# Rolling DVE's and ACT's code of a cached-attention decode kernel into loops, as PE's is

## The chip, the cores and the metric

The kernel runs on one core of a Trainium2 chip. The metric is device time in microseconds for one execution, the median of three runs. A core has five engines that run their own instruction streams and meet through semaphores: PE (TensorE, matrix multiplies), DVE (VectorE), ACT (ScalarE), POOL (GpSimd) and SP (SyncE, which here only issues DMAs). Sixteen DMA engines move data between HBM and the on-chip memory SBUF; a large transfer is split over all sixteen.

## The reference

The reference computes two independent one-token attention blocks, A and B, and concatenates their outputs:

```python
B, Sq, D = 8, 1, 1024;  H, Sk, Dh = 32, 4096, 128
q = (x @ wq).reshape(B, Sq, H, Dh).transpose(0, 2, 1, 3)
scores = einsum("bhqd,bhkd->bhqk", q, k_cache) * Dh ** -0.5
p = softmax(scores, axis=-1)
o = einsum("bhqk,bhkd->bhqd", p, v_cache)
out = o.transpose(0, 2, 1, 3).reshape(B, Sq, H * Dh) @ wo
```

Everything is bf16. The two K caches and the two V caches hold 8 x 32 x 4096 x 128 elements each, 268 MB. Each of them is read once.

## The kernel before

**Slots.** A slot is one batch element b and one group of four heads (`HP = 4`). Eight slots, one for each b, make a group; eight groups (`NG = 8`) make one of the two blocks; so there are 2 x 8 x 8 = 128 slots. For a slot, the K rows of its four heads are one load of 4 MB into one of two buffers `kbuf` (`load_k`, L271), its V rows one load of 4 MB into one of two buffers `vbuf` (`load_v`, L278). Each head takes 32 partitions, and each partition holds 128 of its 4096 positions, 32 KB in one piece.

**What a slot does.** DVE multiplies K by the query in two halves (`multiply`, L315-321, 64 positions of 128 elements for each partition at a time) into `prod`. PE adds up the products by 16 matmuls with an identity (`add_up`, L323) into PSUM, and DVE reduces the last eight columns for each position (`reduce`, L338) into `score`. The softmax is spread over DVE (maximum, L347-352) and ACT (exponentials with their sums, L356). PE multiplies the probabilities with V (`pv`, L370, 32 matmuls), ACT copies the result out of PSUM (L386), PE gathers each head's part (`gather`, L388), and DVE scales it by the inverse sum (`heads`, L399; `invert`, L366) into `on`. Once in a group, `project` (L406) multiplies `on` by the group's four heads of `wo` into the PSUM tile `acc`, and DVE adds that to the running sum `osum` (L418); for a block's last group the sum goes into `orow`, and two small DMAs write it out. Once in a group, too, ACT copies the next group's queries from `qT` into `qg` (`pick_q`, L294), and every four slots PE and ACT spread four queries over the partitions (`make_qbc`, L299).

**The order.** It is written out by hand in one Python loop over n (L435-501). Work of slots n, n-1, n-2 and n-3 is interleaved. Within a pass DVE's order is: first half of the multiply for n, reduce and softmax for n-1, the projection's sum (in passes with n % 8 == 2 and n > 8), second half of the multiply for n, reduce, `heads` of n-2, `invert` of n-1. The K load of slot n+2 needs the buffer of slot n, so it is issued by SP when the second half of the multiply is done; the V load needs the buffer that `pv` has read. All large loads go through SP's queue, in the order of the program. The second block's `wq` takes two turns of the K buffers just before slot 35 (`n == L1`, L443-450): the second of these two loads needs the buffer that slot 34's second multiply reads.

**Semaphores.** `Program.add` records each operation with what it depends on; `Program.finish` (L62) gives each engine's signalled operations consecutive counts and reduces each operation's dependences to waits for counts.

**Loops.** The instruction streams of all engines but PE are straight-line code for all 128 slots. PE alone has loops: slots 3 to 34 (`L0` to `L1`) and 35 to 122 (`L1` to `L2`) repeat every eight slots, so PE runs the first stretch as 4 passes and the second as 11 passes over a body of eight slots (`rolled`, L523). A wait in a body is for a count that rises from pass to pass, held in a register to which a fixed amount is added before the wait. `Program.rolled` (L104) derives these amounts from the recorded waits.

## Time and profile before

| | |
|---|---|
| median of 3 runs | 2588.9 us (2588.84 to 2588.95) |
| profiled execution | 2588.76 us |
| its span, from the first to the last instruction | 2586.4 us |
| mean granted TensorE clock | 0.79 of full speed |
| read from HBM | 1107.33 MB, 428 GB/s over the span |
| DVE first multiply operations (L319) | 256, mean 4.42 us, idle before them 951.9 us in total, for K loads |
| DVE waits ahead of the running sum (L418) | 85.0 us in 14 groups, for PE's projection |
| loads of K: issue to landing, median | 28.5 us |
| loads of V: issue to landing, median | 32.4 us |

The page's busy times are those of an engine's own instructions; register, branch and semaphore instructions and the issue of DMAs are not counted as busy. A share of the DMA engines is the mean over sixteen. The kinds of DMA traffic are told apart by queue: loads and stores that the program issues, and "instruction", by which the engines' own code arrives. All times are on the profiled execution's clock, from the span's start.

### The profile page before, as it was taken

Reading aid. Unit: us, or ns where it says so; the run is one execution under the profiler, and the core shown is the slowest. Engines: PE = TensorE matmul, PEld = TensorE weight load, DVE = VectorE, ACT = ScalarE, POOL = GpSimd, SP = SyncE. Lnnn points to the kernel's source line nnn. Section 1 sums busy time; section 2 is a strip of 40 time slices with the busy share of each in tenths; the row PEclk is TensorE's granted clock in tenths of the full one; section 3 lists DMA queues with packets and bytes.
Section 4 is the critical chain, followed back from the end, with each engine's and each line's share of the span. In section 5 each row is a group of like instructions: output and inputs, shape, how many; then the busy total and the mean of one; then the engine's idle time right before and its main releaser. Section 6 shows DMA issues by size and latency. Waiting matters only on the chain.

```text
span 2586.4 us, 21069 instructions
## 1 busy us (share of the span) xinstructions
PE 1594.8 (62%) x10640; PEld 303.9 (12%) x6800; DVE 1428.3 (55%) x1307; ACT 393.2 (15%) x1201; POOL 1.6 (0%) x11
## 2 busy tenths in 40 slices
PE   4666566556655656666556655665655666655666
PEld 1011111111111111111111111110111101111111
DVE  3655556565545655655556555565655565555555
ACT  0111111111111111111111111111111111111111
POOL 0000000000000000000000000000000000000000
PEclk9778778787877778778877787887877778777788
DMA  9999999999999999999999999999999999999998
GB/s 419 429 431 429 430 431 430 434 432 430 429 412 435 430 430 433 430 431 432 430 431 430 432 431 430 433 430 430 432 430 433 430 431 429 431 432 429 433 432 358
DMA packets 46454, 1107.82 MB, mean 428 GB/s; under 512 B 4512, under 2 KB 4544, under 8 KB 12752
## 3 DMA queue, kind: packets, MB, share of 16 engines
q1 hardware_dynamic: 46336, 1107.32, 99.8%
q8 instruction: 16, 0.26, 0.0%
q14 instruction: 22, 0.18, 0.0%
q10 hardware_dynamic: 80, 0.06, 0.0%
HBM read 1107.33 MB, written 0.03 MB: 428 GB/s over the span
## 4 chain that ended last, share of the span: by engine, by line
DMA 69%; DVE 25%; PE 5%; issue 0%; ACT 0%; SPq 0%
DMA kbuf<-in_A_k_cache_dram 34%; DMA kbuf<-in_B_k_cache_dram 34%; DVE prod L319 22%; PE red L329 4%; DVE score L342 1%; PE acc L413 1%; DMA vbuf<-in_B_v_cache_dram 1%; DVE rmax L347 1%; PE sps L395 1%; DVE tmax L348 0%; DVE nmax L350 0%; DVE osum L418 0%; DVE bias L352 0%; PE oacc L380 0%; PE qps L263 0%
## 5 line engine op out<-in xcount | busy, mean ns | idle before, releaser
L329 PE MATMUL red<-prod,ident 128*128 128x512 bf16 x4096 | 1201.7, 460 | 959.3 <-DVE prod L319 959.1
L319 DVE TENSOR_TENSOR prod<-kbuf,qbc 128x8192 bf16<-128x8192 bf16 x256 | 1131.3, 4420 | 951.9 <-DMA kbuf<-in_A_k_cache_dram 479.6
L356 ACT ACTIVATE prob<-score,bias 32x128 bf16<-32x128 f32 x512 | 295.1, 576 | 1015.6 <-DVE bias L352 1004.6
L386 ACT ACTIVATE osb<-oacc 128x512 f32<-128x512 f32 x128 | 76.4, 597 | 1144.7 <-PE oacc L380 1144.7
L380 PE MATMUL oacc<-vbuf,prob 128*16 128x512 bf16 x4096 | 245.5, 381 | 0.2 <-DMA vbuf<-in_B_v_cache_dram 0.2
L395 PEld LDWEIGHTS sps<-sel,osb 128*128 128x128 f32 x1024 | 135.1, 193 | 632.1 <-issue 431.9
L342 DVE TENSOR_REDUCE score<-red 128x64 f32<-128x512 f32 x256 | 175.3, 685 | 21.5 <-PE red L329 20.6
L380 PEld LDWEIGHTS oacc<-vbuf,prob 128*16 128x16 bf16 x4096 | 90.8, 89 | 565.1 <-issue 473.0
L329 PEld LDWEIGHTS red<-prod,ident 128*128 128x128 bf16 x256 | 33.1, 129 | 1024.9 <-DVE prod L319 1020.1
L356 ACT ACTIVATION_READ_ACCUMULATOR prob<-score,bias 32x1 f32 x512 | 128.0, 250 | 0.0
L395 PE MATMUL sps<-sel,osb 128*128 128x4 f32 x1024 | 122.8, 243 | 1.6 <-ACT osb L386 1.6
L418 DVE TENSOR_TENSOR osum<-acc,osum 40x512 f32<-40x512 f32 x14 | 9.6, 682 | 85.0 <-PE acc L413 85.0
L363 PE MATMUL sps<-rsum,ones 128*128 128x4 f32 x256 | 47.2, 255 | 5.0 <-ACT prob L356 5.0
L363 PEld LDWEIGHTS sps<-rsum,ones 128*128 128x128 f32 x256 | 39.0, 192 | 22.1 <-issue 14.3
L403 DVE TENSOR_TENSOR on<-sps,rl 128x4 bf16<-128x4 f32 x128 | 21.8, 170 | 32.0 <-PE sps L363 17.8
L347 DVE TENSOR_REDUCE rmax<-score 128x1 f32<-128x128 f32 x128 | 36.7, 286 | 4.4
L348 DVE STREAM_TRANSPOSE tmax<-rmax 128x32 f32<-128x32 f32 x128 | 27.1, 212 | 4.4
L350 DVE TENSOR_REDUCE nmax<-tmax 128x1 f32<-128x32 f32 x128 | 23.8, 186 | 4.4
L352 DVE TENSOR_SCALAR bias<-nmax 128x1 f32<-128x1 f32 x128 | 19.7, 154 | 4.4
L368 DVE RECIPROCAL rl<-sps 128x4 f32<-128x4 f32 x128 | 22.0, 172 | 0.0
L269 DVE CAST qT<-qps 128x256 bf16<-128x256 f32 x2 | 0.8, 424 | 35.7 <-PE qps L263 35.7
L312 ACT ACTIVATE qbc<-bps 128x512 bf16<-128x512 f32 x32 | 18.9, 592 | 0.7 <-PE bps L307 0.7
(28 smaller groups left out, 86.3 us busy)
## 6 DMA issues: line engine op xcount, KB each, us to landing
kbuf<-in_A_k_cache_dram SPq DMA_DIRECT2D x64, 4096.0 KB, 28.5
vbuf<-in_A_v_cache_dram SPq DMA_DIRECT2D x64, 4096.0 KB, 32.4
kbuf<-in_B_k_cache_dram SPq DMA_DIRECT2D x64, 4096.0 KB, 28.5
vbuf<-in_B_v_cache_dram SPq DMA_DIRECT2D x63, 4096.0 KB, 32.4
vbuf<-in_A_wq_dram SPq DMA_DIRECT2D x2, 4096.0 KB, 17.5
wob<-in_A_wo_dram SPq DMA_DIRECT2D x8, 1024.0 KB, 30.8
kbuf<-in_B_wq_dram SPq DMA_DIRECT2D x2, 4096.0 KB, 20.2
wob<-in_B_wo_dram SPq DMA_DIRECT2D x8, 1024.0 KB, 30.8
```

The source lines that it names most:

```text
L319: P.add("dve", lambda e: e.tensor_tensor(pv, kv, qbc[:, qi, n % QT, :].unsqueeze(1).to_broadcast([128, CT, Dh]), ALU.mult), reads=[f"k{ki} ...
L329: first = e.matmul(rv, ident[:], pj[:, :, 0, :], start=True, stop=False).ins
L342: P.add("dve", lambda e: e.tensor_reduce(dst, rv, AX.X, ALU.add), writes=[f"score{n % 2}c{ch}"], banks=[f"red{i}"])
L347: P.add("dve", lambda e: e.tensor_reduce(rmax[:, i:i + 1], score[:, i, :], AX.X, ALU.max), reads=sc, writes=[f"rmax{i}"])
L348: P.add("dve", lambda e: e.transpose(tmax[:, i, :], rmax[:, i:i + 1].to_broadcast([128, SEG])), reads=[f"rmax{i}"], writes=[f"tmax{i}"])
L350: P.add("dve", lambda e: e.tensor_reduce(nmax[:, i:i + 1], tmax[:, i, :], AX.X, ALU.max), reads=[f"tmax{i}"], writes=[f"nmax{i}"])
L356: P.add("act", lambda e, pr=pr, hh=hh: e.activation(prob[pr, i, :, hh], score[pr, i, :], ACTF.Exp, bias=bias[pr, i:i + 1], scale=scale, ac ...
L363: P.add("pe", lambda e: e.matmul(sps[:, i * HP:(i + 1) * HP], ones[:], rsum[:, i, :], start=True, stop=True), reads=[f"rsum{i}h{h}" for h ...
L380: last = e.matmul(oacc[i][32 * q:32 * q + TB * HP, :], prob[:, i, j * TB:(j + 1) * TB, :].rearrange("p t h -> p (t h)"), vbuf[:, vi, j * 5 ...
L386: P.add("act", lambda e: e.activation(osb[:, i, :], oacc[i][:], ACTF.Copy), writes=[f"osb{i}"], banks=[f"oacc{i}"])
L395: last = e.matmul(sps[:, o:o + HP], osb[:, i, t * Dh:(t + 1) * Dh], sel[:, t, :], start=(t == 0), stop=(t == TB - 1))
L413: last = e.matmul(acc[32 * half:32 * half + B, :], on[:, hh, :], wob[:, hh, half * 512:(half + 1) * 512], start=(hh == 0), stop=(hh == HP ...
```

## The change

Four things change.

- The loops are kept for each engine in place of PE alone: DVE and ACT, too, run slots 3 to 34 and 35 to 122 as passes over a body of eight slots. `Program.rolled` takes the engine, and now allows for waits whose first pass differs. SP and POOL stay straight.
- What differs from group to group leaves DVE and ACT for GpSimd: the copy of the next queries (`pick_q`), and the running sum of the projections. DVE copies `acc` out of PSUM into a new tile `asb`, and GpSimd copies or adds that to `osum`, now one tile for both blocks. Only the very last projection is still added by DVE.
- `project` moves in the order from ahead of the row-sum matmul and the second multiply to behind the second multiply and its reduce.
- The output of the first block is written from SP's queue in the pass of n = 70; before, it was from ACT's, right behind the block's last projection.

The diff, cut to its core:

```diff
-        self.loops = []
+        self.loops = {e: [] for e in ENGINES}
...
-        pe = self.order["pe"]
-        for a, b, k in self.loops:
...
+        for e in ENGINES:
+            ops = self.order[e]
+            for a, b, k in self.loops[e]:
+                size = (b - a) // k
...
+                for p in range(a, a + size):
+                    if any(ops[p + i * size].sig for i in range(k)):
+                        for i in range(k):
+                            ops[p + i * size].sig = True
...
-    def rolled(self, a, b, k):
-        pe = self.order["pe"]
+    def rolled(self, eng, a, b, k):
+        pe = self.order[eng]
...
+        order = {}
         for p in range(size):
+            for key, v in sorted(value[p].items()):
+                seq = order.setdefault(key, [])
+                if not seq or v > seq[-1][1]:
+                    seq.append((p, v))
+        base, waits = {}, [[] for _ in range(size)]
+        for key, seq in order.items():
+            while seq[0][1] + step[key] <= seq[-1][1]:
+                ahead[key] = max(seq.pop(0)[1], ahead.get(key, 0))
+            was = seq[-1][1] - step[key]
+            base[key] = was
+            for p, v in seq:
+                waits[p].append((key, v - was))
+                was = v
         return ahead, base, waits
...
-        osum = sb("osum", [40, NC, 512], FP32)
+        osum = sb("osum", [40, 512], FP32)
+        asb = sb("asb", [40, 512], FP32)
...
-        P.add("dve", lambda e: e.memset(osum[:], 0.0), writes=["osum0", "osum1"])
...
         def pick_q(gi):
-            P.add("act", lambda e: e.activation(qg[:].rearrange("p h b -> p (h b)"), qT[:, c, g * HP * B:(g + 1) * HP * B], ACTF.Copy),
+            P.add("pool", lambda e: e.tensor_copy(qg[:].rearrange("p h b -> p (h b)"), qT[:, c, g * HP * B:(g + 1) * HP * B]),
...
-            dst, name = (osum, f"osum{c}") if g < NG - 1 else (orow, f"orow{c}")
-            P.add("dve", lambda e: e.tensor_tensor(dst[:, c, :], acc[0:40, :], osum[:, c, :], ALU.add),
-                  reads=[f"osum{c}"], writes=[name], banks=["acc"])
-            if g == NG - 1:
-                for half in range(2):
-                    dma("sp" if c == NC - 1 and half == 0 else "act", out[:, 0, c * D + half * 512:c * D + (half + 1) * 512],
-                        orow[32 * half:32 * half + B, c, :], [f"out{c}{half}"], "out", reads=[name])
+            end = gi == NC * NG - 1
+            dst, name = (osum, "osum") if g < NG - 1 else (orow[:, c, :], f"orow{c}")
+            if end:
+                P.add("dve", lambda e: e.tensor_tensor(dst[:], acc[0:40, :], osum[:], ALU.add), reads=["osum"], writes=[name], banks=["acc"])
+                return
+            P.add("dve", lambda e: e.tensor_copy(asb[:], acc[0:40, :]), writes=["asb"], banks=["acc"])
+            if g == 0:
+                P.add("pool", lambda e: e.tensor_copy(osum[:], asb[:]), reads=["asb"], writes=["osum"])
+            else:
+                P.add("pool", lambda e: e.tensor_tensor(dst[:], asb[:], osum[:], ALU.add), reads=["asb", "osum"], writes=[name])
+
+        def store(c):
+            for half in range(2):
+                dma("sp" if c < NC - 1 or half == 0 else "act", out[:, 0, c * D + half * 512:c * D + (half + 1) * 512],
+                    orow[32 * half:32 * half + B, c, :], [f"out{c}{half}"], "out", reads=[f"orow{c}"])
...
+        def marks():
+            return {e: len(P.order[e]) for e in ("pe", "act", "dve")}
...
             if n == L1 or n == L2:
-                P.loops.append((start, here, (n - L0) // B if n == L1 else (n - L1) // B))
+                for e, at in marks().items():
+                    P.loops[e].append((start[e], at, (n - (L0 if n == L1 else L1)) // B))
...
-                if n - 3 >= 0 and (n - 3) % B == B - 1:
-                    project((n - 3) // B)
             if 0 <= m < NS:
                 rowsum(m)
             if n < NS:
                 multiply(n, 1)
                 reduce(n, 0)
+                if n - 3 >= 0 and (n - 3) % B == B - 1:
+                    project((n - 3) // B)
...
+            if n % (NG * B) == 6 and n > B:
+                store(n // (NG * B) - 1)
+        store(NC - 1)
...
         def run(name, eng):
             ops, at = P.order[name], 0
-            if name == "pe":
-                for a, b, k in P.loops:
-                    straight(name, eng, ops[at:a])
-                    rolled(eng, a, b, k)
-                    at = b
+            for a, b, k in P.loops[name]:
+                straight(name, eng, ops[at:a])
+                rolled(name, eng, a, b, k)
+                at = b
             straight(name, eng, ops[at:])
```

More of the change, by code (lines that the diff above doesn't have):

```diff
@@ L66, in finish @@
                 d.sig = True
-        pe = self.order["pe"]
-        for a, b, k in self.loops:
-            size = (b - a) // k
-            assert size * k == b - a
-            for p in range(a, a + size):
-                if any(pe[p + i * size].sig for i in range(k)):
-                    for i in range(k):
-                        pe[p + i * size].sig = True
+        for e in ENGINES:
+            ops = self.order[e]
+            for a, b, k in self.loops[e]:
+                size = (b - a) // k
+                assert size * k == b - a, (e, a, b, k)
+                for p in range(a, a + size):
+                    if any(ops[p + i * size].sig for i in range(k)):
+                        for i in range(k):
+                            ops[p + i * size].sig = True
         counts = {}
@@ L102, in finish @@
         return counts
-    def rolled(self, a, b, k):
-        pe = self.order["pe"]
+    def rolled(self, eng, a, b, k):
+        pe = self.order[eng]
         size = (b - a) // k
         keys = [sorted(pe[a + size + p].deps) for p in range(size)]
-        step, ahead = {}, {}
+        value, step, ahead = [{} for _ in range(size)], {}, {}
         for p in range(size):
@@ L116, in rolled @@
                 assert pe[a + p].deps.get(key, vals[0] - d) == vals[0] - d, (p, key)
+                value[p][key] = vals[0] - d
             assert all(sorted(pe[a + i * size + p].deps) == keys[p] for i in range(1, k)), p
@@ L119, in rolled @@
             for key, v in pe[a + p].deps.items():
-                if key not in keys[p]:
-                    assert key not in step, (p, key, v)
-                    ahead[key] = max(v, ahead.get(key, 0))
-        last, first, waits = {}, {}, []
-        for p in range(size):
-            w = []
-            for key in keys[p]:
-                v = pe[a + size + p].deps[key] - step[key]
-                if key not in last:
-                    first[key] = last[key] = v
-                    w.append([key, None])
-                elif v > last[key]:
-                    w.append([key, v - last[key]])
-                    last[key] = v
-            waits.append(w)
-        base = {}
-        for w in waits:
-            for x in w:
-                if x[1] is None:
-                    x[1] = first[x[0]] + step[x[0]] - last[x[0]]
-                    base[x[0]] = first[x[0]] - x[1]
-                assert x[1] > 0 and base[x[0]] >= 0
+                if key not in value[p]:
+                    if key in step:
+                        value[p][key] = v
+                    else:
+                        ahead[key] = max(v, ahead.get(key, 0))
+        order = {}
+        for p in range(size):
+            for key, v in sorted(value[p].items()):
[8 more added lines that the diff above has]
+            base[key] = was
+            assert was >= 0
+            for p, v in seq:
+                waits[p].append((key, v - was))
+                was = v
         return ahead, base, waits
@@ L416, in project @@
             P.add("pe", emit, reads=[f"onb{b}" for b in range(B)] + ["wo"], banks=["acc"])
-            dst, name = (osum, f"osum{c}") if g < NG - 1 else (orow, f"orow{c}")
-            P.add("dve", lambda e: e.tensor_tensor(dst[:, c, :], acc[0:40, :], osum[:, c, :], ALU.add),
-                  reads=[f"osum{c}"], writes=[name], banks=["acc"])
-            if g == NG - 1:
-                for half in range(2):
-                    dma("sp" if c == NC - 1 and half == 0 else "act", out[:, 0, c * D + half * 512:c * D + (half + 1) * 512],
-                        orow[32 * half:32 * half + B, c, :], [f"out{c}{half}"], "out", reads=[name])
+            end = gi == NC * NG - 1
[6 more added lines that the diff above has]
+                P.add("pool", lambda e: e.tensor_copy(osum[:], asb[:]), reads=["asb"], writes=["osum"])
+            else:
+                P.add("pool", lambda e: e.tensor_tensor(dst[:], asb[:], osum[:], ALU.add), reads=["asb", "osum"], writes=[name])
[3 more added lines that the diff above has]
+                    orow[32 * half:32 * half + B, c, :], [f"out{c}{half}"], "out", reads=[f"orow{c}"])
         NS = NC * NG * B
@@ L434, in _build @@
         make_qbc(0)
+        def marks():
+            return {e: len(P.order[e]) for e in ("pe", "act", "dve")}
         for n in range(NS + 1):
             m = n - 1
-            here = len(P.order["pe"])
             if n == L0:
-                start = here
+                start = marks()
             if n == L1 or n == L2:
-                P.loops.append((start, here, (n - L0) // B if n == L1 else (n - L1) // B))
+                for e, at in marks().items():
+                    P.loops[e].append((start[e], at, (n - (L0 if n == L1 else L1)) // B))
             second = []
@@ L449, in _build @@
                     q_part(c, s, name, w)
-                start = len(P.order["pe"])
+                start = marks()
             if n < NS:
@@ L521, in straight, with rolled @@
                 one(name, eng, op)
-        def rolled(eng, a, b, k):
-            ahead, base, waits = P.rolled(a, b, k)
+        def rolled(name, eng, a, b, k):
+            ahead, base, waits = P.rolled(name, a, b, k)
             for key, val in ahead.items():
@@ L531, in rolled @@
             with eng.Fori(0, k):
-                for op, ws in zip(P.order["pe"][a:], waits):
+                for op, ws in zip(P.order[name][a:], waits):
                     for key, inc in ws:
@@ L535, in rolled @@
                         eng.wait_ge(sems[key], regs[key])
-                    one("pe", eng, op)
+                    one(name, eng, op)
         def run(name, eng):
             ops, at = P.order[name], 0
-            if name == "pe":
-                for a, b, k in P.loops:
-                    straight(name, eng, ops[at:a])
-                    rolled(eng, a, b, k)
-                    at = b
+            for a, b, k in P.loops[name]:
+                straight(name, eng, ops[at:a])
+                rolled(name, eng, a, b, k)
+                at = b
             straight(name, eng, ops[at:])
```

## The prediction

> **What bounds the kernel now.** I read the page's slices and queues first. In each fence below the first words name the row.

> ```profile
> PE 1594.8 (62%) x10640; PEld 303.9 (12%) x6800; DVE 1428.3 (55%) x1307; ACT 393.2 (15%) x1201; POOL 1.6 (0%) x11
> DMA  9999999999999999999999999999999999999998
> DMA packets 46454, 1107.82 MB, mean 428 GB/s; under 512 B 4512, under 2 KB 4544, under 8 KB 12752
> q1 hardware_dynamic: 46336, 1107.32, 99.8%
> q8 instruction: 16, 0.26, 0.0%
> q14 instruction: 22, 0.18, 0.0%
> ```

> No engine is above 62%, while the loads (q1) fill 16 DMA engines for 99.8% of the span. Then the chain of work that ended last, by engine:

> ```profile
> DMA 69%; DVE 25%; PE 5%; issue 0%; ACT 0%; SPq 0%
> ```

> Its DVE part is only how a K load gets issued: K of slot n+2 is issued 10.4 us after K of slot n has landed (16.4 to 17.8 us in the slots with a projection), and at 10.4 us there are still 18.8 us of earlier loads queued. So DVE, ACT and PE time inside a slot costs nothing. What can move the time is (a) something that occupies a DMA engine, and (b) places where a DMA engine has nothing queued.

> For (a), the two "instruction" rows. The trace's packet records give each fetch a time. The 16 KB ones (q8) are PE's. Of the 22 8 KB ones in q14, ten come every 124 to 132 DVE instructions, nine every 122 to 132 ACT instructions, three every 127 to 129 SP instructions: 8,192 B is 128 instructions. Right after each fetch exactly one load packet is long: normal 32 KB packets take 1.215 to 1.228 us; after a DVE fetch (0.325 us) it is 1.875 us, so that DMA engine loses 0.325 + 0.66 = **1.0 us**; after an ACT or SP fetch 0.31 + 0.38 = 0.7 us; after a PE fetch 1.0 + 0.5, 1.5 to 1.8 in the landings.

> Every load lands in 16 parts, one for each DMA engine. How far the last part is behind the first (my listing of landing events, us):

> ```
> load landed at   last behind first   second-last
>   396.8               2.21              1.80
>   616.0               3.10              1.73
>   725.9               0.41              0.40
>  1142.0               2.38              2.08
>  1438.9               3.39              2.32
>  1665.0               4.42              2.35
>  1961.8               5.42              3.04
>  2187.9               6.42              3.72
>  2465.4               7.42              4.39
>  2577.6 (last wo)     5.02              2.25
> ```

> The last engine steps by 1.0 at DVE's fetches (355, 605, 1125, 1380, 1625, 1877, 2135, 2378 us): all of DVE's code comes through one DMA engine. ACT's comes through another (4.39). A load is complete when its last part is, so the kernel runs at the pace of DVE's DMA engine.

> For (b): the lag collapses at 713 us and shrinks at the end, because the 15 faster engines ran dry there. The gap at 713 comes from slot 34, which holds a projection (time, length, then what DVE waited for):

> ```profile
> 702.65 0.15 DVE L352 TENSOR_SCALAR bias<-nmax 128x1 f32<-128x1 f32 x1
> 709.26 0.68 DVE L418 TENSOR_TENSOR osum<-acc,osum 40x512 f32<-40x512 f32 x1 [6.46 <-PE acc L413]
> 709.87 4.41 DVE L319 TENSOR_TENSOR prod<-kbuf,qbc 128x8192 bf16<-128x8192 bf16 x1
> ```

> ```profile
> 713.00:715.30 2.30, 0.96 (x3) 0.10 (x1) 2.04 (x4) 0.00 (x0) 0.00 (x0) 0.57 0.45 142
> ```

> DVE waits 6.46 us for the projection's matmuls before the second multiply. That multiply frees the buffer of the second wq load, issued at 714.3, while the fast engines finished the first at 713.1 (slowest 716.2). The second fence is the busy time of the stretch 713.0 to 715.3; it ends with PE's clock, the DMA share (0.45) and the rate (142 GB/s).

> **The balance before.** Against a DMA engine that has no fetch and never starves, the end comes late by: starved at 713: 3.1 us (landings 12.8 apart instead of 9.7); starved at 2543: 0.5; starved at 2567, where the last V load waits for K of slot 127 on the slowest engine: 1.9; final lag 5.0. Sum **10.5 us**. Check: 10 DVE fetches x 1.0, plus 0.4.

> **The change, part by part.**

> *DVE and ACT loop.* DVE's 32 + 88 slots become 4 + 11 passes over one body each. A body has 8 x 10 + 1 = 81 operations; the trace shows 8 waits per DVE slot (one K load, three PE, four on itself), so about 68 register adds with those of qbc and the projection, and a branch with its add: about 151 instructions. With 35 ahead, 10 between and 65 behind, DVE's code is about 412 instructions instead of 1,312: 900 fewer, 7 fetches fewer, 3 left. ACT: bodies of 74 operations and 28 for waits and branch; 293 instead of 1,210, 2 fetches left of 9. SP keeps 3, PE its own. If a body stays resident, the lags at the end are then: DVE's engine 0.3 (its lag beside the fetches) + 3 x 1.0 = 3.3; ACT's 0.5 + 2 x 0.7 = 1.9; SP's 0.5 + 2.1 = 2.6; PE's, which go round eight engines (the lengths of the long packets repeat after eight), two fetches each, 3.3 to 3.6. Slowest: 3.4.

> Does a body stay resident? DVE has no loop in this trace; the nearest row is PE's. Its body is 1,067 instructions, over four blocks of 256. Its first pass in the second loop (755 to 911 us) made four q8 fetches; from 915 to 2010, seven passes:

> ```profile
> q1 hardware_dynamic: 19629, 471.74, 100.4%
> q14 instruction: 9, 0.07, 0.0%
> q10 hardware_dynamic: 32, 0.02, 0.0%
> ```

> No q8 row at all: PE loops out of its buffer. (One packet more at 2015, one in eleven passes.) A DVE body of 1.2 of its blocks is smaller by any measure, but its buffer may be smaller too. Bounds: 0 fetches a pass (PE's row), or all of the up to 3 blocks that a body touches, 45 fetches. I take 0, since PE is the only row of a loop. [...]

> *Loop edges.* PE's taken branch lasts 0.208 us, its adds 0.032 each. On DVE and ACT between 0 and, were a fetch waited for, a few us. Cover: DVE idles 8 to 11 us for K in most slots; were that gone, 14 us more are in the queue. Cost 0.

> *Projection behind the second multiply.* In 16 slots K's issue comes back from +17 to +10.4. The cover was there but at slot 34: the second wq goes out at 707.2 instead of 714.3, 5.9 us before the fast engines run out, so the 3.1 us go. Late next is K of slot 35, which waits for PE's q matmuls (726.0), with 9.6 us to spare. The copy of acc behind the reduce costs DVE some 0.68 (the L418 row) ahead of L403 and L368; what waits for those is PE's next slot. Free.

> *GpSimd.* 16 copies of qg, 15 small adds or copies of 40x512. No such POOL row; nearest 0.30 (L217, 128x128). Between 0.1 and, held up for a whole DVE multiply, 5 us each. Slack: qg is used two slots later, osum eight; for the first qg, 29.6 (qbc done) to 33.67 (K lands), 4.1 us, and the queue behind that. Free.

> *Output of the first half from SP* in slot 70: two issues of 0.33 to 0.45 us on SP ahead of K of slot 71, whose wait is longer. Free.

> *The tail* is straight code as before. With a lag of 3.4, V's last load is issued at K127's last landing + 12.6, some 2 us before the fast engines run out: no starving.

> **Sum.** 10.5 - 3.4 = 7.1 us. The profiled execution took 2588.76 (span 2586.42), the median is 2588.9: about **2581.9**. With DVE lags of 2 to 5: 2580.5 to 2584.

> **Rivals.**

> 1. *Slower: bodies are refetched at each taken branch.* Deciding point: 7 refetches more than I count, half a block a pass. One block in 15 passes: DVE's engine lags 0.3 + 18, end 18.3 against 10.5: 2596.7. Two: 33.3, 2611.7. Three: 2627. For it: DVE's buffer is nowhere shown; a body over 151 instructions straddles two or three blocks. Against: PE's loop. 16%.

> 2. *No difference:* the engines share one ceiling, and a pause of one is filled by the others. Then only bytes count: 14 x 8 KB at 431 GB/s, 0.3 us. Against: the lag never shrinks while others idle (5.15 to 5.18 over the last four V parts). Or part of the gain is lost: more code than I count, a body refetched now and then. 2584 to 2592; 12%.

> 3. *The change doesn't do what it says* (the slot-34 gap stays since another wait is behind it): then the engines meet at 713 again, after a gap of the lag there, 2.2 (DVE's engine, two fetches), and the end lag is that of the second half, 2.3. 4.5 against 10.5: 2582.9. Inside the forecast's range.

> **How the numbers follow.** A measurement can tell 0.2%, 5.2 us, from no change. Forecast (with rival 3) 72%, own range 2579.5 to 2584: nearly all of it faster by over 0.2%. Rival 2: same, 12%. Rival 1: slower, 16%. Faster 0.71, same 0.13, slower 0.16. To hold 8 in 10 the range takes in the forecast and rival 2: 2579.5 to 2592; rival 1's prices are left out.

> **What would show it.** Right: q14 down from 22 to about 8; last part at most 4 us behind the first in the last loads; no dip at 713; DVE's wait ahead of L418 gone. Wrong: q14 at 30 or more with long packets every 156 us, or q14 down and the time unchanged (rival 2).

## The result, and the profile after

| | before | after |
|---|---|---|
| median | 2588.9 us (13 runs, 2587.85 to 2592.45) | 2582.25 us (13 runs, 2581.15 to 2585.92) |
| ratio, 95% interval | | 0.9976 [0.9969, 0.9984] |
| profiled execution | 2588.76 us | 2581.38 us |
| its span | 2586.4 us | 2579.6 us |

A second set of eight runs of the changed kernel (e12) gave a median of 2581.68 us, ratio 0.9971 [0.9961, 0.9982]. The executions of the changed kernel fall into two groups, around 2581.5 and around 2585.5 us (nine and four of the thirteen). The kernel before has such a pair too: 66 of its 83 executions on record lie between 2587.8 and 2590.5 us, 17 between 2591.5 and 2594.8. More on that under the runs of the tail.

First the page of the changed kernel: engines, the DMA engines by slice of the span, and the DMA queues.

```profile
PE 1578.8 (61%) x10640; PEld 302.2 (12%) x6800; DVE 1428.6 (55%) x1306; ACT 389.7 (15%) x1185; POOL 21.8 (1%) x42
DMA  9999999999999999999999999999999999999999
DMA packets 46440, 1107.71 MB, mean 429 GB/s; under 512 B 4512, under 2 KB 4544, under 8 KB 12752
q1 hardware_dynamic: 46368, 1107.34, 100.0%
q8 instruction: 16, 0.26, 0.0%
q10 hardware_dynamic: 48, 0.04, 0.0%
q14 instruction: 8, 0.07, 0.0%
```

The engines do the same work in the same time. What differs is q14: 8 fetches of 8 KB in place of 22 (the 32 packets that q1 has more are the first block's output, which q10 has less). By the packet records three are DVE's (105.7, 731.9 and 869.2 us), two ACT's, three SP's. A saving of 14 fetches looks like nothing in this row (0.11 MB of 1107, a share of 0.0%), and it brings nearly all of the result: without the other part of the change (e4, below) the loads still end 5.9 of the 7.3 us earlier.

What the fetches cost is seen in how far the last of a load's sixteen parts lands behind the first. The same reading as in the prediction's listing, of both kernels (us):

```
first part landed   before   after
      396.8          2.21     1.77
      616.0          3.10     1.69
      713.1          3.10     1.68
     1142 / 1139     2.38     3.25
     1439 / 1436     3.39     3.19
     1665 / 1662     4.42     3.16
     1962 / 1959     5.42     3.10
     2465 / 2462     7.42     3.09
     last wo         5.02     3.21
```

The stairs of 1.0 us are gone. The other change is at slot 34, DVE from the end of the softmax on (time, length, operation, then what it waited for), and the stretch at 713 us, whose row ends with PE's clock, the DMA share and GB/s:

```profile
701.24 0.15 DVE L353 TENSOR_SCALAR bias<-nmax 128x1 f32<-128x1 f32 x1
701.31 4.42 DVE L320 TENSOR_TENSOR prod<-kbuf,qbc 128x8192 bf16<-128x8192 bf16 x1
706.29 0.69 DVE L343 TENSOR_REDUCE score<-red 128x64 f32<-128x512 f32 x1 [0.56 <-PE red L330]
708.26 0.68 DVE L423 COPY asb<-acc 40x512 f32<-40x512 f32 x1 [1.28 <-PE acc L414]
```

```profile
713.00:715.30 2.30, 1.07 (x30) 0.56 (x23) 0.00 (x0) 0.60 (x1) 0.00 (x0) 1.00 0.99 427
```

The second multiply starts right behind the softmax, the second `wq` load goes out at 705.8 in place of 714.3, and at 713 the DMA engines move 427 GB/s where they moved 142. The loops' edges cost next to nothing; this is the line of the loop itself, the durations in ns as minimum, median and maximum:

```profile
L547 DVEq COMPARE_BRANCH  x15: 50/56/72, 233.9 to 2467.5; - x15
L547 PEldq COMPARE_BRANCH  x15: 76/208/233, 237.6 to 2471.2; - x15
L547 ACTq COMPARE_BRANCH  x15: 40/45/50, 239.3 to 2472.9; - x15
```

Fifteen branches each, and DVE's and ACT's are shorter than PE's.

### The profile page after: what moved, and what is told of

Same layout as the page of the kernel before. It is cut to its first block, busy times and chain, and to the rows that moved or that the text cites. A ratio compares the mean times of both kernels' runs of the same rounds, so it can differ in the third digit from the quotient of the medians.

```text
span 2579.6 us, 22407 instructions
## 1 busy us (share of the span) xinstructions
PE 1578.8 (61%) x10640; PEld 302.2 (12%) x6800; DVE 1428.6 (55%) x1306; ACT 389.7 (15%) x1185; POOL 21.8 (1%) x42
## 2 busy tenths in 40 slices
DMA packets 46440, 1107.71 MB, mean 429 GB/s; under 512 B 4512, under 2 KB 4544, under 8 KB 12752
## 4 chain that ended last, share of the span: by engine, by line
DMA 73%; DVE 16%; issue 10%; PE 1%; ACT 0%; DVEq 0%; SPq 0%
DMA kbuf<-in_B_k_cache_dram 36%; DMA kbuf<-in_A_k_cache_dram 35%; DVE prod L320 12%; DVE score L343 2%; DMA kbuf<-in_B_wq_dram 1%; DVE rmax L348 1%; DMA vbuf<-in_B_v_cache_dram 1%; DVE tmax L349 1%; DVE nmax L351 0%; PE red L330 0%; DVE bias L353 0%; PE qps L264 0%; PE oacc L381 0%; DVEq L550 0%; ACT prob L357 0%
## 5 line engine op out<-in xcount | busy, mean ns | idle before, releaser
L330 PE MATMUL red<-prod,ident 128*128 128x512 bf16 x4096 | 1188.1, 456 | 963.3 <-DVE prod L320 963.3
L427 POOL TENSOR_TENSOR osum<-asb,osum 40x512 f32<-40x512 f32 x12 | 15.1, 1258 | 1902.8 <-DVE on L404 1902.8
```

Of the source, the lines that this page charges most:

```text
L330: first = e.matmul(rv, ident[:], pj[:, :, 0, :], start=True, stop=False).ins
```

## The experiments

Twelve kernels ran. Times are medians of device time; where a profile decides, the time of the profiled execution is given. Ratios are to the kernel before, run beside each.

### Which part brings the time: four kernels between the two

**e1: ACT's code straight, the rest as changed.** The loops stay planned; only their emission is skipped:

```diff
-            for a, b, k in P.loops[name]:
+            for a, b, k in P.loops[name] if name != "act" else ():
```

> The changed kernel with ACT's code straight again (DVE still in loops). Theory T (each engine's code comes through one DMA engine, and the slowest DMA engine sets the time): nine ACT fetches of 0.7 us and 0.5 beside them put ACT's DMA engine 6.8 us behind at the end, against 3.3 in the changed kernel: profiled execution 2581.4 + 3.5 = 2584.9 us, last part of the late loads about 6.8 us behind the first. Rival B (only bytes count): seven fetches more are 0.06 MB at 431 GB/s, 0.15 us: 2581.5. Rival G (the whole gain is the projection's wait at slot 34, the loops bring nothing): 2581.4.

Measured: 2584.95 us, ratio to the kernel before 0.9985 [0.9976, 0.9994], profiled execution 2584.30. Last part behind the first: 2.3 at 713 us, 3.7 at 1436, 4.5 at 1662, 5.2 at 1959, 5.9 at 2185, 6.6 at 2462: steps of 0.7. For the profiled execution theory T said 2584.9, with a last part 6.8 behind; B and G are 2.8 and 2.9 us too low.

**e2: DVE's code straight, the rest as changed** (`name != "dve"`).

> The changed kernel with DVE's code straight again (ACT still in loops). T: ten DVE fetches of 1.0 us and 0.3 beside them: 10.3 us of lag at the end with nothing to level it at slot 34, so 2581.4 + 7.0 = 2588.4 us, as the kernel before, though the gap at 713 us is gone. B: 2581.5. G: 2581.4.

Measured: 2588.84 us, ratio 0.9998 [0.9989, 1.0007]: no difference from the kernel before. The lag climbs to 4.8 at 1139, 6.8 at 1662 and 9.8 at 2462.

**e3: both straight** (`if name == "pe"`): only the moves of work and of the projection are left.

> The changed kernel with both DVE's and ACT's code straight again: only the moves (queries and sums to GpSimd, projection behind the second multiply, output on SP) are left. T: DVE's DMA engine is the slowest as in the run before, ACT's 6.8 does not count: 2588.4 us, lag 10.3. B: 2581.6. G: 2581.4.

Measured: 2589.03 us, ratio 0.9999 [0.9990, 1.0008]. Its queues, and the stretch at 713 us:

```profile
q14 instruction: 22, 0.18, 0.0%
```

```profile
713.00:715.30 2.30, 2.03 (x33) 0.71 (x32) 0.00 (x0) 0.22 (x1) 0.00 (x0) 1.00 0.96 413
```

All 22 fetches are back, and the gap at 713 us is closed (0.96, 413 GB/s), yet nothing is gained. The lag, which was levelled at 713 us in the kernel before, now runs on to 10.0 at 2462 us. The fastest DMA engine is 3.2 us ahead of where it was (a load whose first part landed at 2465.4 now begins to land at 2462.2), the slowest only 0.5 (its part lands at 2472.3 in place of 2472.8), and the loads wait for that one. This rules out G, and B.

**e4: loops kept, projection back ahead of the second multiply.**

```diff
+                if n - 3 >= 0 and (n - 3) % B == B - 1:
+                    project((n - 3) // B)
             if 0 <= m < NS:
                 rowsum(m)
             if n < NS:
                 multiply(n, 1)
                 reduce(n, 0)
-                if n - 3 >= 0 and (n - 3) % B == B - 1:
-                    project((n - 3) // B)
```

> The changed kernel with the projection back ahead of the row-sum and the second multiply (loops and GpSimd's part kept). T: the gap at 713 us is back, and levels the lag there, some 1.7 to 2.2 us; the end lag is that of the second half, 2.0 to 2.5; together 3.7 to 4.7 against 3.3: 2581.8 to 2582.8 us. G: 2588.4, the time of the kernel before. B: the gap leaves all engines but one without work for 3.1 us: 2584.5.

Measured: median 2584.65 us over 11 runs, spread from 2582.43 to 2587.36, ratio 0.9981 [0.9972, 0.9990]. The profiled execution (2585.83) shows the gap again: two loads begin to land 1.5 us further apart than in a full queue, and the DMA share at 713 us is 0.86:

```profile
713.00:715.30 2.30, 2.30 (x7) 0.00 (x0) 0.36 (x3) 0.00 (x0) 0.88 (x2) 0.50 0.86 299
```

The last `wo` load's last part lands at 2576.7, against 2575.3 in the changed kernel: with loops, the gap costs 1.4 us at the loads. That is T's size at its upper edge (0.4 to 1.4). The other 3 us of this execution came after the last load had landed, from PE's clock (below), so the times alone would not have told it: the median is above the range that T gave, and is the 2584.5 that B gave, which e1 to e3 rule out. Four of the eleven executions are at 2582.4 to 2583.5, at the top of T's range and just above. Why five of them are at 2585.8 or later, more than in the changed kernel, is open.

This order has a second effect, which costs nothing here. GpSimd's sum now runs beside DVE's second multiply and takes 5.37 us each time, where behind the multiply it takes 1.26; its two copies of `asb` take 4.75 in place of 0.61:

```profile
L427 POOL TENSOR_TENSOR osum<-asb,osum x12: 1257/1258/1261, 392.2 to 2468.1; 40x512 f32<-40x512 f32 x12
L427 POOL TENSOR_TENSOR osum<-asb,osum x12: 5365/5372/5374, 391.5 to 2469.4; 40x512 f32<-40x512 f32 x12
```

(Durations in ns, minimum, median and maximum; the changed kernel, then e4.)

Together: closing the gap is worth nothing with DVE's code straight, with ACT's in loops or not (2588.8, 2589.0); with loops it is worth some 1.4 us. The two do not add up; the loops come first.

### What a fetch costs: code added on purpose

**e5: the kernel before, ten tiny instructions more in each slot.** The same edit makes e6, e7, e10 and e11 from the changed kernel, with another PAD:

```diff
+        self.pad = 0
...
-            P.add("dve", lambda e: e.reciprocal(rl[:, i, :], sps[:, i * HP:(i + 1) * HP]), writes=[f"rl{i}"], banks=["sps"])
+            P.add("dve", lambda e: e.reciprocal(rl[:, i, :], sps[:, i * HP:(i + 1) * HP]), writes=[f"rl{i}"], banks=["sps"]).pad = PAD
...
+            for j in range(op.pad):
+                eng.memset(spare[:, j:j + 1], 0.0)
```

> The kernel before with ten tiny DVE instructions more in each slot (memsets of one element of a spare tile, behind the reciprocal, where DVE waits for the next K load anyway): 1,280 instructions, ten blocks of 128. Theory T (each block of DVE's code costs DVE's one DMA engine 1.0 us, and that engine sets the time): 2588.9 + 10 = 2598.9 us, twenty DVE fetches, lag steps of 1.0 twice as often. Rival B (only bytes count): ten times 8 KB at 431 GB/s, 0.2 us: 2589.1. Rival W (DVE's own time): ten times some 0.06 us a slot inside a wait of 8 us: 2588.9.

Measured: 2600.67 us (4 runs; ratio 1.0048 [1.0032, 1.0063]), profiled execution 2598.45, which is 9.7 us above the profiled execution before. Its queues:

```profile
q1 hardware_dynamic: 46336, 1107.32, 99.5%
q8 instruction: 16, 0.26, 0.0%
q14 instruction: 32, 0.26, 0.0%
```

Ten fetches more, 0.97 us each: T's number. B and W are over 9 us too low. The lag climbs in steps of 1.0 as T said, to 5.9 us at 713 and, after the gap there, to 10.1 at 1954; after that it stays between 9.3 and 11.5, as the fast engines then run dry again and again (share 99.5%). The instructions add 16.7 us to DVE's busy time, at places where it waits for K; that this time costs nothing itself is seen in e6, where twice as many a slot cost no more than their fetches. The median lies between two pairs of executions (2598.5 and 2599.0, 2602.4 and 2602.6).

**e6: the changed kernel, PAD = 20.**

> The changed kernel with twenty such instructions more in each slot: a DVE body of 307 instructions, 2.4 blocks, touching three or four; 480 instructions more in all, 3.75 fetches. Q4 (DVE's buffer keeps at least four blocks): only these fetches are added: 2581.4 + 3.8 = 2585.2 us, about seven DVE fetches. Q2 (a window of two blocks): each pass fetches three blocks or more again: 45 fetches or more, lag some 48 us: 2626 us or more.

Measured: 2585.78 us, ratio 0.9987 [0.9977, 0.9996], profiled execution 2585.19. q14 has 12 fetches, seven of them DVE's, as Q4 said. Body of 307 instructions; from 900 to 1250 us, over two passes, its queues have no instruction row at all:

```profile
q1 hardware_dynamic: 6561, 150.76, 100.4%
```

So a body of 307 instructions, 2.4 blocks, is not fetched again over these passes: it stays in DVE's buffer. Q2 is out. Twenty tiny instructions in each slot cost 3.8 us in all, the price of four fetches.

**e10 and e11: PAD = 30 and 40, one execution each.**

> The changed kernel with thirty tiny DVE instructions more in each slot: a DVE body of 387 instructions, 3.02 blocks of 128, touching four; 720 more outside the bodies, 5.6 fetches. R (a body that touches four blocks stays resident): about 9 DVE fetches, 2581.4 + 5.7 = 2587.1 us. N4 (it does not): 15 passes x 4 blocks, about 65 fetches: 2643 us.

> The changed kernel with forty: a DVE body of 467 instructions, 3.65 blocks, touching four or five; 960 more outside the bodies, 7.5 fetches. R: about 11 DVE fetches, 2581.4 + 7.6 = 2589.0 us. N4: one fetch a pass or more, 15 to 75: 2600 to 2665 us.

Measured: 2654.06 and 2662.19 us. Queues of e10, whole span and one pass (1200 to 1360 us):

```profile
q1 hardware_dynamic: 46368, 1107.34, 98.3%
q14 instruction: 79, 0.65, 0.1%
```

```profile
q1 hardware_dynamic: 2789, 66.78, 98.8%
q14 instruction: 6, 0.05, 0.1%
```

Of the 79 fetches five are ACT's and SP's, which leaves DVE 74, about five in each of the 15 passes, one more than the four blocks that the body touches (one comes some 9 us before each branch of the second loop, at 1222.7 and 1385.9 us for the branches at 1231.3 and 1394.9; which block it brings was not shown). That is 71 more than in the changed kernel, for 72.7 us: 1.02 us each. e11: 84 fetches, 76 more, 80.8 us. R fails for both. N4 is right in kind and 11 us short for e10 (four a pass were counted), and e11 came out inside its range only at the upper end.

**e7: PAD = 60.**

> The changed kernel with sixty such instructions more in each slot: a DVE body of 627 instructions, 4.9 blocks, touching five or six; 1,440 more in all, 11.25 fetches. Q6 (the buffer keeps six blocks): 2581.4 + 11.4 = 2592.8 us, about 14 DVE fetches. Q4 (it keeps four or five): every pass fetches its blocks again, 5 x 15 and those outside, some 80 fetches: about 2658 us. Rival W (DVE's own time, 60 x 0.06 = 3.6 us a slot, does it): 3.6 us inside a wait of 8 us, 2581.4.

Measured: 2685.66 us (4 runs), ratio 1.0375 [1.0359, 1.0390], profiled execution 2683.69.

```profile
q1 hardware_dynamic: 46368, 1107.34, 97.7%
q14 instruction: 110, 0.90, 0.1%
```

102 DVE fetches more than in the changed kernel, 102.3 us. The direction is Q4's; its 80 fetches were too few: it counted the five blocks of the body, and a pass of e7 fetches about seven. Q6 and W are out by 91 and 102 us.

DVE's fetches against the profiled execution's time, for the two kernels and those with added code, in one table. The last column is the time above 2581.4 divided by the fetches above three:

| kernel | DVE body | DVE fetches | time, us | us per fetch |
|---|---|---|---|---|
| changed | 147 | 3 | 2581.4 | |
| e6 | 307 | 7 | 2585.2 | 0.95 |
| before | none | 10 | 2588.8 | 1.05 |
| e5 | none | 20 | 2598.5 | 1.00 |
| e10 | 387 | 74 | 2654.1 | 1.02 |
| e11 | 467 | 79 | 2662.2 | 1.06 |
| e7 | 627 | 105 | 2683.7 | 1.00 |

Over thirty times the number of fetches the price stays near 1.0 us. (The rows of before and e5 differ from the changed kernel in more than this, so their last column is a comparison, not a price; e5 less before gives 0.97. Between 3 and 4 fetches the slowest DMA engine changes from one of PE's to DVE's, so that the line needn't begin exactly at three.)

### The two groups of executions: PE's clock in the tail

The executions of the changed kernel that were profiled are of the lower group; e4's profile is of the upper. Stretches of both near the end, each row ending with PE's granted clock, the DMA share and GB/s. The changed kernel, then e4:

```profile
2562.00:2569.00 7.00, 5.76 (x42) 3.19 (x42) 0.36 (x2) 1.06 (x4) 0.00 (x0) 0.52 1.01 422
2569.00:2576.00 7.00, 4.63 (x58) 2.83 (x56) 0.35 (x2) 1.19 (x2) 0.00 (x0) 0.99 0.66 258
```

```profile
2569.00:2576.00 7.00, 6.20 (x56) 2.94 (x48) 0.17 (x1) 0.60 (x1) 0.00 (x0) 0.50 0.78 310
2576.00:2583.00 7.00, 4.25 (x24) 2.14 (x16) 0.86 (x2) 0.60 (x1) 0.00 (x0) 0.50 0.01 2
```

In both, PE's clock falls to 0.5 near its idle stretch ahead of the last row-sum: at 2562.3 us in the changed kernel, whose row-sum starts at 2563.2, and at 2564.8 in e4. In the changed kernel it comes back after 6.83 us, for as long, and falls again at 2576.0; in e4 it stays at 0.5 to the end. The last gather and projection then take 1.84 and 1.87 us in place of 1.03 and 1.40, and the last V products run behind the loads: the end comes 7.3 us after the last landing in place of 4.3. The profile of e3 (2591.99 us) shows the same 0.5 to the end, and 7.8 us. In ten profiles, before, after, e1, e2, e5, e6, e7, e10, e11 and e12, the clock comes back for 6.83 us and the end is 3.8 to 4.7 us behind the last landing. No execution of the kernel before in its upper group was profiled.

**e8: idle matmuls ahead of the last four V parts.**

```diff
+                if len(names) > 1:
+                    def warm(e):
+                        last = None
+                        for _ in range(4):
+                            last = e.matmul(bps[:], ident[:], kbuf[:, 1, 0:512], start=True, stop=True)
+                        return last
+                    P.add("pe", warm, reads=["k1", "ident"], banks=["bps"])
```

> The changed kernel with four idle matmuls (identity times a piece of K, into a bank that is free by then) on PE ahead of each of the last four V parts, while PE waits for them. Theory C (the executions that take 4 us more are those in which PE's granted clock stays at 0.5 through the tail): with PE busy there, the clock comes back: all executions in 2580.8 to 2583 us, the group at 2585.5 gone, median about 2581.4. Rival N (the group comes from the DMA side): a third of the executions stay at 2585.5. Rival L (the idle matmuls get in the way): all 1 to 3 us later.

Measured: 2585.40 us, ratio 0.9987 [0.9978, 0.9996]; eight of eleven executions between 2584.97 and 2585.67, three between 2588.7 and 2589.4. Rival L holds in kind, with 3.6 us in the profiled execution, above its 1 to 3: PE was not waiting there. It came to the first of these parts at 2570.5, some 5 us after it had landed, since the work on slot 126 was still ahead of it, so the four bundles of 1.0 us stood in its way. The theory on the clock isn't tested by this kernel.

**e9: idle matmuls in the idle stretch itself.** The same `warm` with 24 matmuls, ahead of the last row-sum:

```diff
+            if n == NS:
+                P.add("pe", warm, reads=["k1", "ident"], banks=["bps"])
             if 0 <= m < NS:
                 rowsum(m)
```

> The changed kernel with 24 idle matmuls (identity times a piece of K, into a bank that is free by then, some 6 us) in PE's one idle stretch near the end, 7.8 us ahead of the last row-sum, while PE waits for the last softmax. Theory C (the executions that take 4 us more are those in which PE's granted clock, after that stretch, stays at 0.5 to the end): the clock stays at 1.0, the V products and the last gather run at full speed in every execution: all in 2580.5 to 2582.5 us, none at 2585.5, the median up to 0.5 us below the changed kernel's lower group. Rival N (the group comes from the DMA side): a third of the executions stay near 2585.5. Rival L (they get in the way): all 1 to 3 us later.

Measured: 2583.33 us, nine executions from 2581.9 to 2584.41, ratio 0.9976 [0.9966, 0.9986]. Stretches of its profiled execution (2583.47):

```profile
2562.00:2573.00 11.00, 8.03 (x90) 4.39 (x92) 0.53 (x3) 1.98 (x7) 0.00 (x0) 1.00 0.97 398
2573.00:2580.00 7.00, 4.59 (x24) 2.15 (x19) 0.86 (x2) 0.60 (x1) 0.00 (x0) 0.50 0.15 56
```

The clock stays at 1.0 through 2573 as meant, and the 32 V products at 2565.4 take 1.90 us in place of 3.59 in the changed kernel. But PE is then done early, waits for the last V parts (1.90 us ahead of the last), and the clock falls to 0.5 at 2573.0, in time for the last gather and projection (1.84 and 1.87 us). No execution is in the upper group, and two (2581.90 and 2582.23) are within the lower one's range and C's; the other seven lie between the groups. So filling PE's idle time ahead of the tail moves the clock, and the clock moves the end: by 1.8 us in this profile (span 2581.4 against 2579.6), by 3.1 in e4's. N's third near 2585.5 did not come, though nine executions are few: five of the changed kernel's 21 are there. The gain that C expected did not come either: the fall was moved, not removed.

**e12: the changed kernel again, beside e9.**

> The changed kernel as it is, beside the 24-matmul kernel on the same chip: median 2582, nine in thirteen executions near 2581.5 and the others near 2585.5, as in its first runs.

Measured: 2581.68 us, eight executions, seven from 2581.1 to 2582.1 and one at 2585.8.

## Why the prediction was right

**The bound.** "The kernel runs at the pace of DVE's DMA engine" is what e2 and e3 show (no gain while DVE's code is straight, whatever else is removed) and what e5 prices from the other side (ten fetches, 9.7 us).

**The sizes of the code.** Forecast bodies of 151 and 102 instructions; measured 147 and 94, with 65 register adds in DVE's where 68 were counted. Fetches left: 3, 2 and 3 for DVE, ACT and SP, each as forecast.

**The lag at the end.** Forecast 3.4, carried by PE's engines; measured 3.1 to 3.3 over the last loads. Nine engines stand between 2.7 and 3.3 us at the last load, as two PE fetches each, or DVE's three, make them.

**Residence of the body**, which was the open cost: none of DVE's blocks is fetched again in the changed kernel. That it stays was right; the ground for it was thin, one row of another engine with blocks of another size, and how far DVE's body was from the edge was not known. e6 and e10 now give it: 307 instructions stay, 387 do not. Rival 1's mechanism is real, its deciding point is a body between these two, and its price might have been higher than any that it named: e10's passes fetch about five blocks, where rival 1 went up to three.

**Rival 3**, the gap at slot 34 that stays, is what e4 builds. Priced at a gap of 2.2 and an end lag of 2.3, it measured 1.5 and 2.2 (3.2 after PE's fetch at 2558.5 us), and its 2582.9 us is met by e4's four early executions.

**Loop edges, GpSimd, output.** 0.056 and 0.045 us for a branch; 1.26 us for GpSimd's sum and 0.21 for its copy of the queries, inside the bounds of 0.1 to 5, though only in this order: beside a DVE multiply the sum takes 5.37 (e4), above the bound; DVE's time before and after 1428.3 and 1428.6 us. All free, as forecast.

**The tail.** No landing late: the last V load was issued at 2555.5, and the first of its four pieces begins to land 2.5 us behind the load ahead, as in a full queue. Slowest landing 7.3 us earlier than before, end of the span 6.8 us: the difference is the last projection, 1.40 us in place of 1.03, on PE's clock.

**The sum.** Forecast 2581.9, 7.1 us less; the profiled executions differ by 7.4, the medians by 6.7 and, in the second set, 7.5.

What was loose: the text spoke of slot 34 as a term ("so the 3.1 us go"). In the balance this is right, but as the worth of that edit it isn't: alone it brings nothing (e3), and with loops 1.4 us (e4), because a gap that levels the DMA engines takes away as much lag as it costs. And PE's clock in the tail was not thought of at all. Five of the changed kernel's 21 executions take 4 us more, over half of the gain; that the clock goes with them too is an estimate from the profiles of e3 and e4, as none of the five was profiled. In the listing the second-last part of the load at 1438.9 is 2.01 behind the first, not 2.32; nothing rests on it.

What a block of code costs shows on the DMA engine that brings it: 0.97 us each in e5. The prediction took PE's loop as its ground, and that was a weak point: PE's body of 1,067 instructions is not fetched again (no q8 row over seven passes, from 915 to 2010 us), while a DVE body of 387 is, in every pass (e10). So PE's row says nothing on DVE's buffer. How much that buffer holds was not shown beyond this: a body of 2.4 blocks stays (e6), one of 3.0 does not (e10).

## What to carry to other kernels

When the DMA engines are full, ask which of the sixteen is last: list the landings of a load's parts, and see whether the distance between first and last grows. Straight-line code is itself a load, and all of one engine's code may come through one DMA engine, as DVE's and ACT's did here, so a 0.0% row can set the time. Rolling DVE's loop paid with a body that stayed in its buffer (147 instructions, and 307 in e6); one of 387 cost ten times what that had saved (72.7 us in e10, against 7.4). And see whether the slowest DMA engine is idle in a gap before closing it: closing the one at slot 34 brought nothing with DVE's code straight (e3), and 1.4 us with loops (e4).
